# Filter loads moved to the software DMA queue behind a gate, and block 1 normed by a matmul broadcast, in an FFT mixing and SwiGLU kernel

## Chip, cores, metric

The kernel runs on one core of one Trainium2 chip. The metric is device time in microseconds (us); lower is better. All timed comparisons are of fast-state runs.

Engines are named as in the profile: PE is TensorE (PEld its weight loads), DVE VectorE, ACT ScalarE, POOL GpSimd, SP SyncE, which here only issues DMAs. A "q" after an engine (SPq, POOLq) is its sequencer. DMA queue q1 is the hardware queue of SyncE, q0 the software queue of GpSimd's DMAs; q8 and q14 are those that the DMA views mark "instruction": they carry instruction fetches. In the code, psb is the result of B, psi that of its inverse, and pg the first gate matmul's: "first pg" is where the main loop begins.

## The reference, cut to what matters

```python
X = np.fft.rfft(x, axis=1)              # x: 8 batches, 3008 tokens, 256 channels
F = (filt_r + 1j * filt_i)[None, :, :]  # 1505 frequencies x 256 channels, fp32
y = np.fft.irfft(X * F, n=x.shape[1], axis=1)
x = y.reshape(B * S, D)                 # 24064 tokens
rms = np.sqrt(np.mean(x * x, axis=-1, keepdims=True) + 1e-06)
xn = x / rms * rms_g
g = xn @ w_gate                         # 256 -> 1536
out = (g / (1 + exp(-g)) * (xn @ w_val)) @ w_out
```

## The kernel before

The transform is done as small matrix products in four steps (A, B with the filter, its inverse, and the inverse of A). Between A and B, and again before the last step, data bounces through DRAM to change its layout: `z_store` writes, `t2_load` reads a "bounce tile" of 8 of the 32 frequency groups. Batch 0 is transformed in a prologue in which nothing else can run. Batches 1 to 7 are transformed inside the gate/value/down matmuls of the batch ahead of them, from a list of slots.

The filters come in four chunks. Each chunk has a real and an imaginary part of 64 x 2048 fp32 in partitions 0 to 63, of which only rows 0 to 23 and 32 to 55 are filled, and is then copied to partitions 64 to 127:

```python
def f_load(c):
    for src, dst in ((filt_r, fr), (filt_i, fi)):
        t = dst[c]
        nc.sync.dma_start(t[0:24, :, :]..., raw(src, c * KC, [[64 * D, 24], [1, KC * D]]))   # 8 KB rows
        lo = 1 if c == 0 else 0
        for a, e in ((0, 16), (16, 23)):                                # 1 KB rows, backwards
            nc.sync.dma_start(t[32 + a:32 + e, lo:KC, :], raw(src, ..., [[64 * D, e - a], [-D, KC - lo], [1, D]]))
        ...
def f_dup(c):
    nc.vector.tensor_copy(out=fr[c][HALF:P], in_=fr[c][0:HALF])
    nc.scalar.activation(out=fi[c][HALF:P], in_=fi[c][0:HALF], func=AXT.Copy)
```

The mixing loop of batch 0 has 16 units. Unit i multiplies by the filter on VectorE if i is even, on GpSimd if i is odd:

```python
# b_unit (cut): psb = wb @ t2, then the products with fr and fi
eng = nc.vector
if b == 0 and i % 2:
    eng = nc.gpsimd            # ScalarE first copies psb to SBUF, as v
eng.tensor_tensor(out=s1, in0=ps, in1=f1, op=ALU.mult)
eng.tensor_tensor(out=s2, in0=ps, in1=f2, op=ALU.mult)

# the order of issue after the z stores (cut)
nc.sync.dma_start(wi[:, 0], wi0_d)
f_load(0); t2_load(0, 0); t2_load(0, 1); f_load(1); t2_load(0, 2); f_load(2)
...
for i in range(19):
    if i < 16: b_unit(0, i)
    if i == 5: t2_load(0, 3); f_load(3)
    if i == 9: w_load(0)                       # FFN weights, on GpSimd
    if i % 4 == 1 and i // 4 + 1 < NC: f_dup(i // 4 + 1)
    if i >= 3: bi_unit(0, i - 3)               # psi = wi @ products
    ...
```

Block 0 of the first batch is normed by a matmul that broadcasts its scale. Block 1, like all others, sends its scale to DRAM and back (`rho_move`), and GpSimd multiplies (`xn_unit`).

## Time and profile before

The time is 1011.37 us (median of 3 runs, 1011.34 to 1012.87).

| stage | from, us | to, us | what it is |
|---|---|---|---|
| x loads, step A, z stores | 1 | 18.5 | DMA engines 90% busy, 212 GB/s |
| filters and tiles arrive, mixing loop | 19 | 73.3 | TensorE busy for 21.0 of 54.3 us |
| bounce, first norm | 73.3 | 86.4 | TensorE busy for 3.5 of 13.1 us; the longest wait, 6.4 us, is for a bounce load |
| main loop | 86.4 | 1009.9 | TensorE dense (895.8 of 923.5 us) |

This is the windows view of the kernel before: stretch and its length in us, busy us of each engine with its number of instructions, the granted clock of TensorE (PEclk, 1.00 is full), the mean busy share of the DMA engines, and what they moved.

```profile
core 0: us, PE busy (x) PEld busy (x) DVE busy (x) ACT busy (x) POOL busy (x), PEclk, DMA share, GB/s
19.00:32.00 13.00, 0.92 (x6) 0.70 (x7) 6.81 (x10) 3.29 (x4) 0.00 (x0) 0.50 1.06 140
32.00:45.00 13.00, 4.34 (x20) 2.46 (x19) 4.40 (x6) 2.36 (x2) 2.48 (x2) 0.50 0.93 112
45.00:56.00 11.00, 4.30 (x19) 2.68 (x19) 3.23 (x4) 6.05 (x10) 6.28 (x5) 0.50 0.86 131
56.00:74.00 18.00, 11.42 (x59) 7.47 (x56) 7.48 (x9) 10.50 (x17) 14.80 (x13) 0.72 0.73 133
74.00:86.00 12.00, 3.05 (x30) 2.56 (x31) 2.15 (x6) 1.08 (x2) 7.22 (x11) 0.60 0.81 177
```

No engine is busy for much more than a third of 32 to 45 us (4.40 of 13), but the DMA engines are at 93%, and they move only 112 GB/s.

The timeline of the kernel before gives the steps (start in us, duration, engine, line, operation, output<-inputs; in brackets the idle time of the engine and what ended it):

```profile
23.43 0.32 SPq L205 DMA_DIRECT2D t_241<-z_tmp  x1
...
31.68 1.87 PE L212 MATMUL psb<-t_241,wb 96*128 96x256 f16 x8 [11.94 <-DMA t_241<-z_tmp]
...
39.27 1.22 DVE L423 COPY fr_115<-fr_115 64x2048 f32<-64x2048 f32 x1 [5.67 <-DMA fr_115<-in_filt_r_dram]
...
43.24 1.91 ACT L424 ACTIVATE fi_119<-fi_119 64x2048 f32<-64x2048 f32 x1 [9.91 <-DMA fi_119<-in_filt_i_dram]
...
61.53 1.91 ACT L424 ACTIVATE fi_121<-fi_121 64x2048 f32<-64x2048 f32 x1 [3.52 <-DMA fi_121<-in_filt_i_dram]
...
73.00 0.27 PE L238 MATMUL psi<-hh,wi 128*128 128x256 f16 x1
...
86.40 1.18 PE L365 MATMUL pg<-xn,wg 128*128 128x512 f16 x2
...
107.07 0.59 PE L365 MATMUL pg<-xn,wg 128*128 128x512 f16 x2 [1.99 <-POOL xn L345]
```

The first bounce tile is used at 31.68 us. fr_115 and fi_119 are chunk 1, fi_121 is the imaginary part of chunk 3: their copies wait for the loads (VectorE stood idle for 5.67 us and ScalarE for 9.91 us before those of chunk 1), and what follows them in the program waits too (TensorE 8.52 us before the psi at 46.30 us). The mixing loop ends at 73 us, the main loop begins at 86.40 us, and at 107.07 us there is one stall of 1.99 us for block 1.

One more view should have been weighed harder before predicting. It is the DMA view of the kernel before, 21 to 24 us, when only filter rows of chunk 0 were on the way (the first bounce tile is issued at 23.43 us, and none of its packets starts before 24):

```profile
DMA packets 270, 0.35 MB, mean 115 GB/s; under 512 B 51, under 2 KB 253, under 8 KB 253
...
q1 hardware_dynamic: 270, 0.35, 97.9%
```

With the hardware queue 98% busy, 115 GB/s passed. (Stretches such as 39 to 43 us, in which only filter rows are issued, don't serve: 315 of their 526 packets are 512 B rows of a bounce tile issued at 31.66 us.)

### The profile page before, as it was taken

How to read it: one execution, taken by the hardware profiler on the slowest of the kernel's cores; microseconds unless marked ns; L12 is line 12 of the kernel's file. 1: busy time of each engine (PE TensorE's matmuls, PEld its weight loads, DVE VectorE, ACT ScalarE, POOL GpSimd, SP SyncE). 2: the span in 40 equal slices, each digit the busy share in tenths (PEclk: the TensorE clock that was granted, in tenths of full speed). 3: DMA queues.
4: the chain of work that ended last, by engine and by line, in shares of the span. 5: the costliest groups of instructions: out<-in, count | busy, mean ns of one | idle time of the engine just before them, and what ended most of it. 6: DMA issues, size and time to landing. Idle time of an engine off the chain costs nothing.

```text
span 1009.9 us, 17370 instructions
## 1 busy us (share of the span) xinstructions
PE 927.2 (92%) x6279; PEld 568.1 (56%) x6279; DVE 592.3 (59%) x969; ACT 607.6 (60%) x1063; POOL 246.7 (24%) x205
## 2 busy tenths in 40 slices
PE   2257979999999999999999999999999999999997
PEld 1134546655665566655665566655665566656663
DVE  7233468546774477545774477645775467645554
ACT  6254745676655865566655765667656765566543
POOL 1264331033301341032401232031411322033300
PEclk8567999999999999999999999999999999999999
DMA  8979564425632474335723374324724353312211
GB/s 188 117 136 187 131 141 86 121 74 114 148 101 72 108 162 94 100 76 137 150 70 99 94 163 112 99 66 112 160 71 123 87 129 85 106 44 61 44 41 40
DMA packets 95879, 107.24 MB, mean 106 GB/s; under 512 B 16944, under 2 KB 70770, under 8 KB 95602
## 3 DMA queue, kind: packets, MB, share of 16 engines
q1 hardware_dynamic: 87362, 91.26, 36.1%
q0 software_dynamic: 8336, 14.68, 9.9%
q8 instruction: 49, 0.80, 0.3%
q14 instruction: 36, 0.29, 0.1%
q10 hardware_dynamic: 96, 0.20, 0.1%
HBM read 70.88 MB, written 49.90 MB: 120 GB/s over the span
## 4 chain that ended last, share of the span: by engine, by line
PE 73%; DMA 7%; ACT 4%; issue 3%; DVE 3%; POOL 1%; SPq 1%; ACTq 0%; DVEq 0%; POOLq 0%
PE pg L365 21%; PE pv L365 20%; PE psi L238 5%; PE psb L212 3%; PE psn L270 1%; ACT sq L279 1%; SPq L201 1%; PE psa L191 1%; DMA wv<-in_moe_w_val_dram 1%; ACT y L277 1%; PE psq L287 1%; DMA r_tmp<-rho 1%; DVE hh L370 1%; ACT sg L369 1%; PE po_12770 L382 0%
## 5 line engine op out<-in xcount | busy, mean ns | idle before, releaser
L370 DVE TENSOR_TENSOR hh<-pv,sg 128x512 f16<-128x512 f32 (+1 forms) x576 | 391.0, 679 | 349.9 <-ACT sg L369 226.7
L369 ACT ACTIVATE sg<-pg 128x512 f16<-128x512 f32 (+1 forms) x576 | 340.6, 591 | 309.1 <-PE pg L365 305.3
L365 PE MATMUL pg<-xn,wg 128*128 128x512 f16 (+1 forms) x1152 | 339.9, 377 | 2.0 <-POOL xn L345 2.0
L365 PE MATMUL pv<-xn,wv 128*128 128x512 f16 (+1 forms) x1152 | 338.9, 376 | 0.0
L382 PEld LDWEIGHTS <-hh 128*128 128x128 f16 (+1 forms) x2304 | 221.4, 98 | 112.0 <-issue 34.0
L345 POOL TENSOR_TENSOR xn<-y,rb 128x1024 f16<-128x1024 f32 (+1 forms) x47 | 129.6, 2758 | 314.8 <-DMA rb<-r_tmp 265.9
L365 PEld LDWEIGHTS <-wv 128*128 128x128 f16 x1152 | 113.0, 98 | 132.0 <-issue 1.9
L299 POOL TENSOR_TENSOR rho<-u,mhalf 128x4 f32<-128x4 f32 x48 | 48.8, 1016 | 337.7 <-DVE u L297 322.4
L365 PEld LDWEIGHTS <-wg 128*128 128x128 f16 x1152 | 105.7, 98 | 24.4 <-issue 2.7
L238 PEld LDWEIGHTS <-wi 128*128 128x128 f16 x512 | 51.8, 102 | 55.6 <-issue 17.3
L277 ACT ACTIVATE y<-psn,gsb 128x512 f32<-128x512 f32 (+1 forms) x94 | 64.3, 684 | 10.1 <-PE psn L270 4.8
L279 ACT ACTIVATE sq<-psn 128x512 f16<-128x512 f32 (+1 forms) x94 | 55.6, 591 | 0.0
L212 PEld LDWEIGHTS <-wb 96*128 96x128 f16 x256 | 24.8, 105 | 47.5 <-issue 21.8
L191 PE MATMUL psa<-xc,wa 128*128 128x512 f16 x96 | 36.6, 393 | 11.1 <-DMA xc<-in_x_dram 9.2
L175 POOL DMA_DIRECT2D xc<-in_x_dram x64 | 34.9, 554 | 6.0 <-DMA wo<-in_moe_w_out_dram 2.7
L238 PE MATMUL psi<-sg,wi 128*128 128x256 f16 x32 | 12.1, 381 | 18.2 <-ACT t_350 L243 8.5
L287 PEld LDWEIGHTS <-sq 128*128 128x128 f16 (+1 forms) x384 | 17.5, 97 | 11.7 <-ACT sq L318 0.9
L191 PEld LDWEIGHTS <-wa 128*128 128x128 f16 x96 | 9.2, 99 | 18.1 <-issue 8.3
L287 PE MATMUL psq<-ones,sq 128*128 128x1 f16 (+1 forms) x384 | 17.5, 165 | 0.6 <-ACT sq L318 0.6
L238 PE MATMUL psi<-hh,wi 128*128 128x256 f16 x32 | 12.0, 380 | 1.5 <-POOL hh L230 1.5
L212 PE MATMUL psb<-t_241,wb 96*128 96x256 f16 x8 | 1.9, 415 | 11.9 <-DMA t_241<-z_tmp 11.9
L435 DVE TENSOR_SCALAR wi<-pst 64x512 f16<-64x512 f32 (+1 forms) x16 | 10.7, 671 | 2.4 <-ACT wi L433 2.1
(900 smaller groups left out, 1140.1 us busy)
## 6 DMA issues: line engine op xcount, KB each, us to landing
rb<-r_tmp SPq DMA_DIRECT2D x47, 256.0 KB
xc<-in_x_dram POOLq DMA_DIRECT2D x56, 192.0 KB, 6.1
xc<-in_x_dram POOLq DMA_DIRECT2D x8, 160.0 KB, 6.6
wb<-wb_t SPq DMA_DIRECT2D x4, 192.0 KB
wg<-in_moe_w_gate_dram POOLq DMA_DIRECT2D x3, 256.0 KB, 5.7
wv<-in_moe_w_val_dram POOLq DMA_DIRECT2D x3, 256.0 KB, 7.5
wo<-in_moe_w_out_dram POOLq DMA_DIRECT2D x3, 256.0 KB, 9.2
r_tmp<-rho SPq DMA_DIRECT2D x47, 2.0 KB
```

Source lines behind the costliest of these rows:

```text
L191: nc.tensor.matmul(ps, wa, st[b]["x"][c][:, 2 * r:2 * r + 2, :], start=True, stop=True)
L212: nc.tensor.matmul(ps[:, u, :], wb[:, k, :], st[b]["t2"][k // KC][:, k % KC, :], start=True, stop=True)
L238: nc.tensor.matmul(ps[:, u, :], wi[:, 2 * i + u, q, :], s12[q][:, u, :], start=(q == 0), stop=(q == 1))
L277: nc.scalar.activation(out=y[:, dh, 0:w], in_=ps[:, 0:w], func=AXT.Identity, scale=gsb[:, dh:dh + 1])
L279: nc.scalar.activation(out=st[b]["sq"][m][:, dh, 0:w], in_=ps[:, 0:w], func=AXT.Square)
L287: nc.tensor.matmul(ps[0:w, q:q + 1], sq[:, dh, q * P:q * P + w], ones, start=(dh == 0), stop=(dh == 1))
L299: nc.gpsimd.tensor_tensor(out=rho, in0=u, in1=mhalf, op=ALU.pow)
L345: nc.gpsimd.tensor_tensor(out=xv[:, :, 0:nq], in0=yv[:, :, 0:nq], in1=rv[:, 0:nq].unsqueeze(1).to_broadcast([P, 2, nq, P]), op=ALU.mult)
L365: nc.tensor.matmul(ps[:, 0:w], wt[:, dt_, ts(jt, P)], xn[:, dt_, 0:w], start=(dt_ == 0), stop=(dt_ == 1))
L369: nc.scalar.activation(out=sg[:, 0:w], in_=pg[:, 0:w], func=AXT.Silu)
L370: nc.vector.tensor_tensor(out=hh[:, 0:w], in0=pv[:, 0:w], in1=sg[:, 0:w], op=ALU.mult)
L382: nc.tensor.matmul(po[s4 // 2][0:w, s4 % 2, :], hh[:, s4 * P:s4 * P + w], wo[:, jt, :], start=(jt == 0 and s4 % 2 == 0), stop=(jt == JT - ...
```

## The change

Its intent: chunk 0 goes out early, behind the x loads, so that the first bounce tile finds an empty queue; chunks 1 and 2 wait (a "gate", a one-element copy on GpSimd) for that tile to land, so that they don't take its bandwidth; units 1 and 3 leave GpSimd, which is issuing then; and block 1 gets the matmul broadcast of block 0, without a trip through DRAM. The core of the diff:

```diff
-        if b == 0 and i % 2:
+        if b == 0 and i % 2 and i > 4:
             eng = nc.gpsimd
@@ f_load: all its DMAs
-            nc.sync.dma_start(...)
+            nc.gpsimd.dma_start(...)
@@ before step A
+        f_load(0)
@@ after the z stores
+        for c in range(3):
+            t2_load(0, c)
+        gate(st[0]["t2"][0][0:1, 0, 0:1])
+        f_load(1)
+        f_load(2)
         nc.sync.dma_start(wi[:, 0], wi0_d)
-        f_load(0)
-        t2_load(0, 0)
-        t2_load(0, 1)
-        f_load(1)
-        t2_load(0, 2)
-        f_load(2)
@@ mixing loop
-            if i % 4 == 1 and i // 4 + 1 < NC:
+            if i % 4 == 2 and i // 4 + 1 < NC:
                 f_dup(i // 4 + 1)
@@ block 1
-        at(2, rho_move, 0, 1)
-        at(7, xn_unit, 0, 1)
+        at(3, scale_split, 1)
+        at(5, scale_apply, 1, 0)
```

`scale_split` and `scale_apply` are the code that block 0 had already, cut in two: the scale is split in two fp16 parts, 8 small matmuls broadcast it, and VectorE multiplies.

More of the change, by code (lines that the diff above doesn't have):

```diff
@@ L321, in norm_first, with scale_split @@
         st[0]["sq"][0] = sq
+        st[0]["y"][0] = y
         q_unit(0, 0)
-        rho = st[0]["u"].pop(0)
+        scale_split(0)
+        scale_apply(0, 1)
+    def scale_split(m):
+        rho = st[0]["u"].pop(m)
         hl = up.tile([P, 2, 4], FP16, tag="hl", name="hl")
@@ L326, in norm_first, with scale_apply @@
         nc.vector.tensor_tensor(out=hl[:, 1, :], in0=rho, in1=hl[:, 0, :], op=ALU.subtract)
-        ps = bank(1, "psr")
+        st[0]["u"][m] = hl
+    def scale_apply(m, bk):
+        hl = st[0]["u"].pop(m)
+        y = st[0]["y"].pop(m)
+        ps = bank(bk, "psr")
         for q in range(4):
@@ L334, in norm_first @@
             nc.vector.tensor_tensor(out=xn[:, dh, :], in0=ps, in1=y[:, dh, :], op=ALU.mult)
-        st[0]["xn"][0] = xn
+        st[0]["xn"][m] = xn
     def xn_unit(b, m):
@@ L411, in f_load @@
             t = dst[c]
-            nc.sync.dma_start(t[0:24, :, :].rearrange("p a d -> p (a d)"),
+            nc.gpsimd.dma_start(t[0:24, :, :].rearrange("p a d -> p (a d)"),
                                 raw(src, c * KC, [[64 * D, 24], [1, KC * D]]))
@@ L415, in f_load @@
             for a, e in ((0, 16), (16, 23)):
-                nc.sync.dma_start(t[32 + a:32 + e, lo:KC, :],
+                nc.gpsimd.dma_start(t[32 + a:32 + e, lo:KC, :],
                                     raw(src, 64 * (a + 1) - c * KC - lo,
@@ L419, in f_load @@
             if c == 0:
-                nc.sync.dma_start(t[32:56, 0, :], raw(src, 32, [[64 * D, 24], [1, D]]))
+                nc.gpsimd.dma_start(t[32:56, 0, :], raw(src, 32, [[64 * D, 24], [1, D]]))
     def f_dup(c):
```

## The prediction

> **What bounds the kernel now.** The timeline shows two regimes. From the first gate/value matmul (86.4 us) to the end (1009.9 us) TensorE is dense: 689.5 us busy of 700 between 300 and 1000 us (windows view). Before 86 us TensorE is mostly idle (0.9 us busy of 13 between 19 and 32 us, 5.0 of 15 between 32 and 47). So the change can win only in the prologue, about microsecond for microsecond, plus a 2.0 us stall at 107.07 us, where pg waits for GpSimd's xn of block 1.
>
> **Why the prologue is slow.** All filter chunks and bounce tiles stand in one line on the SyncE queue. Filter chunk 0 is issued from 19.08 to 22.13 us, so the first bounce tile is issued at 23.43 and first used at 31.68 us. Chunk 1 is then behind two tiles: its real part is duplicated at 39.27, its imaginary part at 43.24 us; chunk 2 at 49.39/52.00, chunk 3 at 59.38/61.53. Each late chunk stops VectorE or ScalarE and then TensorE (waits of 8.5, 5.0, 4.5 us before psi). The mixing loop runs from 31.68 to 73.3 us; its undisturbed pace (55 to 59 us) is 1.28 us a unit, 21 us for 16. DMA engines are about 90 to 100% busy from 19 to 52 us but move only 107 to 149 GB/s.
>
> **What changes.**
> - Chunk 0 is issued by GpSimd from about 5.8 us, behind the x loads, and competes with the z stores (up to 18.5 us). It lands by about 20 us, the z stores 1 to 2 us later than now. The first tile then has an empty queue (4.2 us in the steady state): first used at 26.5 to 27.5.
> - Chunks 1 and 2 are released by that landing: 12 issues of about 0.55 us (as an x load). [...] The trace has both queues busy at 80 to 86 us (71% and 37%)[...]. Chunk 1 about 33 to 36, chunk 2 about 39 to 41, chunk 3 about 48 to 52 us.
> - Units 1 and 3 go to VectorE: +2 x 1.37 us there, -2 x 2.5 us on GpSimd. wi's first slice now lands behind three tiles, about 36 us, and holds the first psi.
> - From then GpSimd limits: units 5 to 15 are 6 x 2.5 us, with about 3.5 us for chunk 3's issues and 2.3 us for w_load between them. Last unit about 60 us instead of 72.7.
> - Block 1's scale: removed: the DRAM round trip (5.65 + 3.22 us) and the 2.88 us GpSimd multiply; added: 8 small matmuls (0.5 to 0.9 us), two VectorE multiplies (1.3 us). The 2.0 us stall goes; net about -1.3 us.
>
> **Sum.** About 11 us from the mixing loop, 1 from block 1: 999.5 us (-1.2%). Range 992 to 1007. Faster by over 2%: 0.07; within 2%: 0.91; slower: 0.02.
>
> **What would show it.** Right: first psb at 26 to 28 us; chunk-1 copies before 37; last psi near 60 to 63; first pg near 74 to 76; no pg wait for GpSimd at block 1. Wrong: psb still near 31, or copies moving under 5 us.
>
> **What would make it wrong.** Filter rows slower on the software queue; chunk 0 delaying x or z; chunk 3's issues blocking GpSimd's units; rho of block 1, behind GpSimd's x issues, stalling VectorE at slot 3.

About 11 us and 1 us off the 1011.4 us measured before come to about 999.5 us.

## The result, and the profile after

The changed kernel took 1010.05 us (median of 4 runs, 1009.26 to 1011.88), the kernel before 1011.57 us in the same comparison. The ratio is 0.9985, with a 95% interval of 0.9968 to 1.0002. A ratio here is the mean time of one kernel's fast runs over that of the other's of the same rounds, so it isn't quite the ratio of the medians. The gain is 1.5 us where 12 were forecast, and 1010 lies outside the stated range.

The windows view of the kernel after, the same stretches:

```profile
19.00:32.00 13.00, 3.75 (x24) 2.72 (x24) 9.93 (x16) 3.97 (x5) 4.34 (x7) 0.50 0.95 203
32.00:45.00 13.00, 3.72 (x17) 2.44 (x18) 4.45 (x7) 3.47 (x4) 4.13 (x7) 0.50 0.83 99
45.00:56.00 11.00, 8.03 (x38) 5.02 (x36) 6.20 (x8) 5.74 (x8) 10.91 (x12) 0.50 0.79 154
56.00:74.00 18.00, 7.75 (x37) 4.47 (x35) 4.25 (x5) 8.60 (x13) 10.62 (x10) 0.59 0.62 125
74.00:86.00 12.00, 7.51 (x49) 4.33 (x50) 4.00 (x9) 4.41 (x8) 8.24 (x13) 0.50 1.10 211
```

From 19 to 32 us more is moved (203 instead of 140 GB/s) and TensorE does more. From 32 to 45 us it is worse than before: 99 GB/s, and TensorE is busy for 3.72 of 13 us. The timeline of the kernel after:

```profile
27.64 1.86 PE L212 MATMUL psb<-t_240,wb 96*128 96x256 f16 x8 [4.93 <-DMA t_240<-z_tmp]
...
37.46 1.22 DVE L433 COPY fr_115<-fr_115 64x2048 f32<-64x2048 f32 x1 [4.81 <-DMA fr_115<-in_filt_r_dram]
...
41.44 1.91 ACT L434 ACTIVATE fi_119<-fi_119 64x2048 f32<-64x2048 f32 x1 [15.97 <-DMA fi_119<-in_filt_i_dram]
...
57.57 1.91 ACT L434 ACTIVATE fi_121<-fi_121 64x2048 f32<-64x2048 f32 x1 [5.17 <-DMA fi_121<-in_filt_i_dram]
...
68.39 0.27 PE L238 MATMUL psi<-hh,wi 128*128 128x256 f16 x1
...
81.94 1.18 PE L375 MATMUL pg<-xn,wg 128*128 128x512 f16 x2
```

The first tile is used 4.0 us sooner (27.64 for 31.68), as forecast. But chunk 1's copies come only 1.8 us sooner, and ScalarE stood still for 15.97 us before the imaginary one. The main loop begins at 81.94 instead of 86.40 us: 4.5 us gained, where about 11 were forecast. The line of pg at block 1 with its wait for GpSimd is gone.

This is the DMA view of the kernel after, 32 to 36 us. In this stretch no other queue moved anything (size of each DMA, and us from issue to landing, in the issue lines):

```profile
DMA packets 159, 0.39 MB, mean 97 GB/s; under 512 B 87, under 2 KB 87, under 8 KB 136
...
q0 software_dynamic: 159, 0.39, 95.1%
...
fr_116<-in_filt_r_dram POOLq DMA_DIRECT2D x1, 192.0 KB, 11.1
...
fi_119<-in_filt_i_dram POOLq DMA_DIRECT2D x1, 56.0 KB, 9.8
```

Filter rows alone on the DMA engines: 97 GB/s with the engines 95% busy, and 9 to 11 us from issue to landing, which includes the time behind the rows issued earlier. On the hardware queue it was 115 GB/s, in packets of 1 and 8 KB (202 and 17, beside 51 of under 512 B) where the software queue's are of 4 and 8 KB (49 and 23, beside 87 of under 512 B). The rows are slow on either queue, somewhat slower on the software queue.

### The profile page after: what moved, and what is told of

It reads as the page before. It is cut to its first block, busy times and chain, and to the rows that moved or that the text cites. A ratio compares the mean times of both kernels' runs of the same rounds, so it can differ in the third digit from the quotient of the medians.

```text
span 1007.4 us, 17371 instructions
## 1 busy us (share of the span) xinstructions
PE 930.0 (92%) x6287; PEld 569.4 (57%) x6287; DVE 596.2 (59%) x977; ACT 606.2 (60%) x1061; POOL 255.0 (25%) x227
## 4 chain that ended last, share of the span: by engine, by line
PE 76%; DMA 9%; ACT 5%; issue 4%; DVE 2%; POOL 2%; SPq 1%; ACTq 0%; DVEq 0%; POOLq 0%
PE pg L375 21%; PE pv L375 20%; PE psi L238 5%; PE psb L212 3%; PE psn L270 2%; ACT sq L279 1%; PE psa L191 1%; SPq L201 1%; DMA fi_119<-in_filt_i_dram 1%; DMA xc<-in_x_dram 1%; PE psq L287 1%; ACT y L277 1%; DMA fi_120<-in_filt_i_dram 1%; DMA fi_121<-in_filt_i_dram 1%; DVE hh L380 0%
## 5 line engine op out<-in xcount | busy, mean ns | idle before, releaser
L355 POOL TENSOR_TENSOR xn<-y,rb 128x1024 f16<-128x1024 f32 (+1 forms) x46 | 126.8, 2757 | 315.3 <-DMA rb<-r_tmp 243.5
L212 PEld LDWEIGHTS <-wb 96*128 96x128 f16 x256 | 25.0, 105 | 41.4 <-issue 17.7
L191 PE MATMUL psa<-xc,wa 128*128 128x512 f16 x96 | 36.5, 393 | 12.1 <-DMA xc<-in_x_dram 9.7
L191 PEld LDWEIGHTS <-wa 128*128 128x128 f16 x96 | 9.2, 99 | 18.5 <-issue 8.7
L445 DVE TENSOR_SCALAR wi<-pst 64x512 f16<-64x512 f32 (+1 forms) x16 | 10.7, 672 | 5.4 <-ACT wi L443 5.2
```

Source lines behind the costliest of these rows:

```text
L191: nc.tensor.matmul(ps, wa, st[b]["x"][c][:, 2 * r:2 * r + 2, :], start=True, stop=True)
L212: nc.tensor.matmul(ps[:, u, :], wb[:, k, :], st[b]["t2"][k // KC][:, k % KC, :], start=True, stop=True)
L355: nc.gpsimd.tensor_tensor(out=xv[:, :, 0:nq], in0=yv[:, :, 0:nq], in1=rv[:, 0:nq].unsqueeze(1).to_broadcast([P, 2, nq, P]), op=ALU.mult)
```

## Experiments

The theory: the filter rows themselves land slowly, so an earlier or freer queue only moves their start. The first rival: GpSimd's issuing and its share of the products limit the loop. A second question is where the rest went, because the main loop after the first pg got longer: 923.5 us before and 925.5 after, though a stall of 2 us had been taken out of it. (The second traces, below, gave 925.5 and 926.3 us: the kernel before alone scattered by 2 us here, so the lengthening itself is no larger than the scatter. What didn't come is a shortening by the stall's 2 us.)

### The two kernels again

No edit; new runs and a second trace of each.

> The changed kernel again, for a closer time and a second trace. Theory A (the prologue saved about 5 us, and the tile waits of the seven later batches differ from run to run): ratio 0.996 to 0.999, first pg again near 82 us, but the sum of TensorE's waits for bounce tiles after that (13.8 us in the first trace, 11.1 before) comes out different, anywhere from 10 to 15 us. Rival (the change makes the later waits longer): the sum is again 13 us or more, and the waits are the same ones.

> The kernel before against itself. Ratio 1.000 within 0.1%. A second trace shows by how much the waits of the later batches scatter with nothing changed: theory A expects their sum (11.1 us in the first trace) to move by 1 to 3 us; the rival expects it to stay at 11 us within 0.5.

The changed kernel took 1008.12 us (6 runs) beside 1012.69 us for the kernel before (11 runs): ratio 0.9959 (0.9939 to 0.9978). The kernel before against itself gave 1.0004 (0.9986 to 1.0022). So the change is a small gain, 0.15% in the first comparison and 0.4% in this one, with runs that scatter over some 4 us. In the second traces first pg is at 80.07 (after) and 86.32 us (before), 6.3 us apart. TensorE's waits for bounce tiles in batches 1 to 7 sum to 14.9 us (13.8 in the first trace) after and 12.1 us (11.1) before. Scatter within one kernel is about 1 us, the lower edge of what the theory had expected and over the rival's 0.5, but the kernels differ by 2.7 us both times. So the theory's hope that this was scatter fell, and the rival ("the change makes later waits longer") stood. It is taken up below.

### Filter bytes cut to an eighth

```diff
+        if c:                 # chunks 1 to 3: as many DMAs, one column of 8 (wrong result, on purpose)
+            for src, dst in ((filt_r, fr), (filt_i, fi)):
+                for p, r, e in ((0, 0, 24), (32, 1, 16), (48, 17, 7)):
+                    nc.gpsimd.dma_start(dst[c][p:p + e, 0, :], raw(src, 64 * r + c * KC, [[64 * D, e], [1, D]]))
+            return
```

> The changed kernel with the same number of filter issues, but an eighth of the bytes in chunks 1 to 3 (result wrong on purpose). Theory A (the bytes of the filter rows land slowly, about 97 GB/s with an otherwise empty queue, and that takes back what the earlier start gave): the copy of chunk 1's imaginary part moves from 41.4 to about 34 us, the last psi from 68.4 to about 60 to 62, first pg from 82 to about 74 to 76. Rival B (GpSimd's issuing and its share of the products limit the loop, whatever the bytes): first pg moves by less than 2 us.

The result is wrong. The time was 1001.0 us, ratio 0.988 (0.9855 to 0.9905). Chunk 1's imaginary copy came at 33.73 us. Timeline of this run:

```profile
59.60 0.42 PE L238 MATMUL psi<-hh,wi 128*128 128x256 f16 x1
...
73.58 1.18 PE L375 MATMUL pg<-xn,wg 128*128 128x512 f16 x2
```

With seven eighths of the bytes gone and every issue still there, the loop ended 8.8 us and the main loop began 8.4 us sooner than in the first trace of the change (6.7 and 6.5 us sooner than in the second), within half a microsecond of where the prediction had put them (60 to 63 and 74 to 76 us). The missing part of the mixing loop's gain is thus the landing of the filter rows; this run cuts bytes and the number of rows together, and the next two tell them apart. In this run GpSimd's chain of products and issues ran almost without a break from 37.4 to 59.2 us, so the rival is right about what limits next, not about what limited here.

### The imaginary part through the other half of the partitions

```diff
-        for src, dst in ((filt_r, fr), (filt_i, fi)):
-            t = dst[c]
+        for src, dst, o in ((filt_r, fr, 0), (filt_i, fi, HALF)):
+            t = dst[c][o:o + HALF]
@@ f_dup
-        nc.scalar.activation(out=fi[c][HALF:P], in_=fi[c][0:HALF], func=AXT.Copy)
+        nc.scalar.activation(out=fi[c][0:HALF], in_=fi[c][HALF:P], func=AXT.Copy)
```

(The zeros that are set before the load move too.)

> The changed kernel with the imaginary filters loaded into partitions 64 to 119 and copied down, instead of loaded into 0 to 55 and copied up; same bytes, same issues, same queue. Theory A1 (the rows land slowly because real and imaginary part go to the same few partitions[...]): rate in the stretch with only filters moving rises from 97 to 130 to 180 GB/s, chunk 1's imaginary copy at about 37 to 39 us instead of 41.4, last psi 2 to 4 us earlier. Rival A2 (small rows or the software queue itself limit): nothing moves by more than 1 us.

DMA view of this run, 32 to 36 us, again only filter rows:

```profile
DMA packets 216, 0.56 MB, mean 140 GB/s; under 512 B 108, under 2 KB 108, under 8 KB 187
...
q0 software_dynamic: 216, 0.56, 90.6%
...
fr<-in_filt_r_dram POOLq DMA_DIRECT2D x1, 192.0 KB, 7.2
fi<-in_filt_i_dram POOLq DMA_DIRECT2D x1, 192.0 KB, 6.8
```

The same bytes from the same queue with the same issues pass at 140 instead of 97 GB/s, because half of them go to other partitions: separate DMAs to the lower and the upper half added up in part here, to 1.44 times the rate. Chunk 1's imaginary copy came at 37.59 us (it then waited for VectorE, no longer for the load), last psi at 63.65, first pg at 77.34 us, 4.6 and 2.7 us sooner than in the two traces of the change. The time was 1005.44 us, ratio 0.9937 (0.9906 to 0.9968); this interval overlaps that of the change (0.9939 to 0.9978), so it is the trace that shows the gain. The rival, that small rows or the software queue limit (nothing moving by more than 1 us), falls.

What is shown is that other partitions helped. Why they helped isn't shown, for no run separates the possible causes.

### Half the bytes: filters cast to fp16 on the way in

```diff
-    fr = [glob.tile([P, KC, D], FP32, ...
-    fi = [glob.tile([P, KC, D], FP32, ...
+    fr = [glob.tile([P, KC, D], FP16, ...
+    fi = [glob.tile([P, KC, D], FP16, ...
```

> The changed kernel with filters cast to fp16 on the way in: same rows and partitions, half the bytes written. If the bytes into the few partitions limit, chunk 1's imaginary copy comes at about 36 to 37 us instead of 41.4 and first pg at about 76 to 78. If the number of rows (descriptors) limits, the copies move by under 1 us. Result should stay within tolerance.

The result is correct. The time was 998.42 us, ratio 0.9859 (0.9842 to 0.9876), against 0.9959 for the change alone: this one edit on top of the change gains more than twice what the change did. Chunk 1's imaginary copy came at 34.12 and first pg at 71.39 us, both sooner than the 36 to 37 and 76 to 78 expected. DMA view of this run, 30 to 34 us, only filter rows:

```profile
DMA packets 694, 0.37 MB, mean 94 GB/s; under 512 B 258, under 2 KB 652, under 8 KB 694
...
q0 software_dynamic: 694, 0.37, 90.7%
...
fr<-in_filt_r_dram POOLq DMA_DIRECT2D x1, 96.0 KB, 4.8
fi<-in_filt_i_dram POOLq DMA_DIRECT2D x1, 96.0 KB, 3.4
```

The rate in bytes that arrive is the same as with fp32 (94 and 97 GB/s), but half as many have to arrive, and they land in 3 to 5 instead of 9 to 11 us. There were more than four times as many packets in 4 us (694 for 159), so packets or rows are not what was short. Together with the run before, the bytes written into few partitions limited (97 and 94 GB/s into the lower half alone, 140 into both). (Not all of the gain is landing: fp16 also shortens VectorE's copies, 0.69 for 1.22 us, and the products on GpSimd, 1.15 for 1.26 us each, and the first psb came sooner, at 25.7 us.)

### Without the gate

```diff
-        gate(st[0]["t2"][0][0:1, 0, 0:1])
-        f_load(1)
-        f_load(2)
@@ before step A
         f_load(0)
+        f_load(1)
+        f_load(2)
```

> The changed kernel without the gate: chunks 1 and 2 are issued by GpSimd right after chunk 0, from about 14.6 us. If the rows' own slowness is what costs and they can share the engines with z stores and tiles, chunk 1's imaginary copy comes at 28 to 32 us instead of 41.4, the first psb at 29 to 32 instead of 27.6, first pg at 75 to 79 us. If early filters only take from z stores and tiles what they gain (the reason for the gate), the first psb comes after 33 and first pg stays at 80 to 83.

Timeline of this run:

```profile
38.32 1.87 PE L212 MATMUL psb<-t,wb 96*128 96x256 f16 x8 [9.78 <-DMA t<-z_tmp]
...
83.44 1.18 PE L375 MATMUL pg<-xn,wg 128*128 128x512 f16 x2
```

The filters were early, and the z stores and the first tile paid: the last z store was issued by 27.8 instead of 22.2 us, the first psb came 10.7 us later than with the gate, first pg at 83.44 us. The time was 1009.27 us, ratio 0.9974 (0.9951 to 0.9996). So the gate does what it is for in the prologue, and of the two outcomes set out above, the two streams didn't share well (from 20 to 24 us both queues were busy, q1 71.3% and q0 36.9%, and 180 GB/s passed). In time it isn't told apart from the change (0.9939 to 0.9978): the intervals overlap.

### The two parts apart

```diff
# filter_only: the change, but block 1 as before
-        at(3, scale_split, 1)
-        at(5, scale_apply, 1, 0)
+        at(2, rho_move, 0, 1)
+        at(7, xn_unit, 0, 1)
# norm_only: the kernel before, with the opposite edit (and scale_split, scale_apply)
```

> The change without its second part: filters on the software queue, block 1 normed through DRAM as before. If the two parts add: first pg at 80 to 82 us, the 2.0 us wait of pg for GpSimd is back, and the time is 1 to 1.5 us over the full change's. On the later batches (waits for the first bounce tile of batches 2 to 7, 9.4 and 9.9 us with the change, 6.5 and 7.6 before): if the shifted queues of SyncE and GpSimd (26 fewer issues on one, 22 to 23 more on the other) cause the longer waits, the sum here is 9 us or more; if block 1's norm causes them, it is 6.5 to 7.6.

> The kernel before with the matmul broadcast for block 1 alone. Prologue unchanged: first pg at 86.3 to 86.5 us; the wait of pg for GpSimd at block 1 gone; first batch's bounce-tile wait ends 1.2 us sooner after first pg. If the TensorE clock is then low for 6.8 us instead of 3.4 after that wait, as in all traces with the change, the second part is worth nothing: ratio 0.999 to 1.0005. Waits of batches 2 to 7: see filter_only, the other way round.

The filter part alone: 1008.61 us, ratio 0.9952 (0.9932 to 0.9972), as good as the whole change (0.9959). The norm part alone: 1014.3 us, ratio 1.0012 (0.9995 to 1.0029). Its first pg came at 87.72 us where 86.3 to 86.5 were expected of an unchanged prologue: a prologue, too, scatters by over 1 us from trace to trace. So the second part is worth nothing in time, although its trace shows the stall of 2 us at block 1 gone. My guess that a longer stretch of low clock after batch 1's tile wait eats it was wrong: that stretch was 3.4 us with the norm part alone and 6.8 us with the filter part alone. (In the trace of the norm part alone the clock was at 0.50 for another 3.4 us, from 817.0 us, right behind the last batch's wait; in the first traces of the two kernels it stayed at 1.00 there. Whether that recurs isn't shown.)

The waits for the first tile of batches 2 to 7 sum to 7.5 us with the filter part alone and 8.8 us with the norm part alone, which points to the norm. What differs most is the last batch. Its wait for the first bounce tile is 2.8 us with the norm part alone, 0.8 us with the filter part alone. The timeline of the kernel before, where the last batch's first tile is issued and used:

```profile
812.96 0.32 SPq L205 DMA_DIRECT2D t_10466<-z_tmp  x1
...
816.39 0.38 PE L212 MATMUL psb<-t_10466,wb 96*128 96x256 f16 x2 [1.22 <-DMA t_10466<-z_tmp]
```

The same in the kernel after:

```profile
809.18 0.32 SPq L205 DMA_DIRECT2D t_10474<-z_tmp  x1
...
814.22 0.38 PE L212 MATMUL psb<-t_10474,wb 96*128 96x256 f16 x2 [2.48 <-DMA t_10474<-z_tmp]
```

And the DMA view of the kernel after between the two, where the queue that fetches instructions shows up:

```profile
q8 instruction: 1, 0.02, 2.2%
```

One 16 KB fetch, 1.8 us on one DMA engine (2.2% of 16 engines over 5.1 us), falls inside the tile's load. The same view of the kernel before, 812.9 to 816.4 us, has no q8, but it has a smaller fetch on q14, of 8 KB:

```profile
q14 instruction: 1, 0.01, 0.9%
```

So not every fetch lengthens the load: with this one inside it took 3.4 us, and 3.7 us in the second trace of the kernel before, also with an 8 KB fetch of q14 inside. The fetches meant below are those of q8. In the main loop they come about 19 us apart (47 between 110 and 990 us of the kernel before), in which TensorE runs some 250 matmuls and weight loads (12,216 in 923.5 us). The DMA views don't say whose instructions they carry; that they are TensorE's was the guess. The next two runs add TensorE instructions alone and show whether the fetches move with them. The norm by matmul adds 16 TensorE instructions, at that rate about 1.2 us of the fetch's position (an estimate).

### Moving the instruction fetch

```diff
# before_pad16: the kernel before; prologue matmuls of wi_group done twice where TensorE idles
         for a in range(lo, 4):
-            nc.tensor.matmul(ps[:, a, :], wb[:, 4 * g + a, :], ident[0:KR, :], start=True, stop=True)
+            for _ in range(2 if g >= 6 else 1):
+                nc.tensor.matmul(ps[:, a, :], wb[:, 4 * g + a, :], ident[0:KR, :], start=True, stop=True)
# after_pad80: the kernel after, with range(3 if g >= 4 else 2 if g >= 2 else 1)
```

> The kernel before, with 8 matmuls of the prologue done twice (TensorE idles there): 16 more TensorE instructions, exactly what block 1's norm by matmul adds, and nothing else. In all seven traces with the matmul norm, a 16 KB instruction fetch falls 1 to 3 us after the issue of the last batch's first bounce tile, that tile takes 4.8 to 5.7 us from issue to use and TensorE waits 2.2 to 3.1 us; in the three without, the fetch falls outside it, the tile takes 3.4 to 3.7 and the wait is 0.8 to 1.5. If the position of the fetch does it, this kernel shows the fetch inside, a tile of 4.8 us or more and a wait over 2 us. If the new data path of block 1 does it (rival), the wait stays at 0.8 to 1.5 us.

> The changed kernel, with 40 matmuls of the prologue done twice or thrice: 80 more TensorE instructions, so that each fetch comes about 5.9 us sooner (about 13.6 instructions a us). Fetch theory: the fetch leaves the load of the last batch's first tile (it comes 4 to 5 us before its issue), the tile takes 3.4 to 3.8 us again and the wait is 0.8 to 1.6 us instead of 2.5 and 2.7. Rival: wait still over 2.2 us.

(The trace of the kernel before has 8,888 matmuls and weight loads from 150 to 809 us, 13.5 a us; by that, too, 80 are 5.9 us, an estimate.)

Both are single looks of unknown state; only the traces are compared, for the last batch's first tile:

| kernels | q8 instruction fetch | issue to use, us | TensorE's wait, us |
|---|---|---|---|
| 3 traces without the matmul norm | outside the load | 3.4 to 3.7 | 0.8 to 1.5 |
| 9 traces with it | 0.9 to 2.7 us after issue | 4.8 to 5.7 | 2.2 to 3.1 |
| before_pad16 | 0.8 us after issue | 4.1 | 1.9 |
| after_pad80 | 4.3 us ahead of issue | 3.5 | 1.7 |

(The 9 are all runs with the matmul norm, other than after_pad80.) Sixteen more instructions, where TensorE idles, brought the fetch into the tile's load (from 4.4 and 5.0 us after issue in the two traces of the kernel before; more than the 1.2 us expected) and lengthened it by 0.4 to 0.7 us, less than the 1.1 us or more that I expected. This alone would prove little: batch 4's first tile took 4.1 and 4.3 us in the two traces of the kernel after with no fetch inside. Eighty took it out again and the load was 3.5 us, where all nine others had 4.8 or more. The fetch moved with TensorE's instructions both times. So its position is shown to lengthen this load, by one trace in each direction. The whole of the longer wait isn't shown: 1.9 us is under the 2 us expected, 1.7 is over the 0.8 to 1.6. In after_pad80 fetches came near other batches' first tiles instead, whose waits rose: batch 1 to 6.6 us (4.4 and 5.0 in the traces of the kernel after), batch 5 to 1.8 (1.1 and 0.9), batch 6 to 2.7 (1.2 and 1.1). Only in batch 5 did the fetch fall inside the load. In batches 1 and 6 it came 3.5 and 4.4 us ahead of the issue, and the load of batch 6 was no longer for it (3.65 us; 3.63 and 3.54 in those traces), so how the wait rose there stays open. The cost moves about rather than going away.

### Candidates to beat both

```diff
# combo: imaginary part through the upper half, as above, and
-        if b == 0 and i % 2 and i > 4:
+        if b == 0 and i % 3 == 2 and i > 4:
@@ chunk 3 right behind chunk 2 instead of in unit 5
         f_load(2)
+        f_load(3)
@@
                 t2_load(0, 3)
-                f_load(3)
# combo16: the same with fp16 filters
```

> A candidate to beat both: imaginary filters through the upper partitions, chunk 3 issued right after chunk 2 (GpSimd idles there), and every third unit instead of every second on GpSimd. If GpSimd's chain limits once the rows land sooner, the last psi comes at 56 to 58 us instead of 63.65 (imaginary filters moved alone) and first pg at 70 to 72, time about 1001 us. If the landing of rows still limits, last psi stays over 61.

> The candidate with fp16 filters on top: imaginary filters through the upper partitions, chunk 3 right after chunk 2, every third unit on GpSimd. fp16 alone gave first pg at 71.4 us, limited by GpSimd's chain from then on. If that chain is what is left, last psi at 51 to 55 us, first pg at 65 to 69 us, time 991 to 996 us. If neither bytes nor GpSimd bind any more, first pg stays near 71.

The fp32 candidate missed: last psi at 60.66 and first pg at 74.49 us (expected 56 to 58 and 70 to 72), 1002.5 us, ratio 0.9881 (0.9858 to 0.9905). Chunk 3 landed late (its imaginary copy began at 49.61 us), so the rows probably still limited; but 60.66 lies just under the 61 us set for that reading, so this run alone doesn't show it. With fp16 the expectation held: last psi at 53.49 us, and in the timeline

```profile
67.30 1.18 PE L375 MATMUL pg<-xn,wg 128*128 128x512 f16 x2
```

The time was 993.39 us (5 runs, 990.56 to 995.61) beside 1012.93, ratio 0.981 (0.9786 to 0.9834), with a correct result. It is the best kernel and beats the kernel before and the changed one.

## Why the prediction was wrong, point by point

- **Right: what bounds.** Only the prologue could win, and the first tile's use at 26.5 to 27.5 us came at 27.64 and 27.37 us in the two traces, within 0.2 us.
- **Slightly off: the z stores.** They were put 1 to 2 us later. The last was issued by 22.2 instead of 18.5 us, because the second half of the wb load was held up on SyncE (issued at 16.73 instead of 13.79 us), and the stores behind it with it. It did no harm, for the first tile was issued at 23.84 us (23.43 before).
- **Wrong, and the main error: "Chunk 1 about 33 to 36, chunk 2 about 39 to 41, chunk 3 about 48 to 52 us."** The copies came at 37.5 and 41.4 (chunk 1), 46.8 (chunk 2), 55.5 and 57.6 us (chunk 3). The step assumed that the rows had been slow because of what stood in front of them on one queue. They were slow by themselves: 115 GB/s on the hardware queue, 97 on the software queue. With an eighth of the bytes the rest of the forecast came true (59.6 and 73.6 us); this term is 8.4 us at first pg against the first trace of the change and 6.5 us against the second. The prediction had named "filter rows slower on the software queue" as a way to fail. That is at most the smaller part: by these two rates the 0.75 MB of chunk 1 would land about 1 us sooner on the hardware queue (an estimate), where its imaginary part came 5.4 and 3.5 us after the forecast's 36 in the two traces. No run gated the rows on the hardware queue, so the share of the queue isn't measured.
- **Mis-sized for it: "About 11 us from the mixing loop".** Measured 4.5 and 6.3 us at first pg, in two pairs of traces.
- **Right, but later: "From then GpSimd limits".** GpSimd's chain from unit 5 took 23.0 us (45.08 to 68.11) where the terms of the prediction sum to 20.8. It began about 6 us later than a last unit at 60 us implies (39.2), because chunk 1 was late; with few filter bytes it began at 37.36 us.
- **Wrong in effect: "1 from block 1".** The stall went, as forecast, but the time didn't (1.0012 alone, and 0.9959 with against 0.9952 without). One part of the return was found: the last batch's tile load was over 1 us longer in the nine traces in which the matmul norm had moved an instruction fetch into it. The rest is within the scatter of runs and stays open.
- The chance of 0.91 for "within 2%" was right. The range of times had no room for a wrong idea of why the rows were slow.

## What to carry to other kernels

When DMA engines are over 90% busy at about half of the throughput that they reach elsewhere in the same trace (here 115 GB/s, and 207 at 80 to 86 us of the kernel before), look at where the bytes land before moving them to another queue: here other partitions gave 1.44 times the rate, half the bytes less than half the time to land (3 to 5 for 9 to 11 us), another queue nothing (97 for 115 GB/s). Before crediting a reorder with the whole of a wait, find a stretch of the old trace in which only that traffic moves (by its packets, not only by what is issued in it), and take its own rate as the floor. And a saving of 1 us in the middle of a dense loop should be timed alone: it may be given back far away from it, as at the last batch's tile here.
